# Attention division in two operations with its product on VectorE or ScalarE, the turned x of sequences 2 and 3 by DMA, the scale in the keys, and a new instruction order

## The chip, the cores and the metric

The kernel runs on one core of one Trainium2 chip. The metric is device time in microseconds (us). The kernel before takes 217.81 us, the median of 3 runs (217.51 to 218.0).

The engines of the core each work through a list of instructions in order and wait for one another at semaphores: PE (TensorE: matrix products and turns), DVE (VectorE), ACT (ScalarE), POOL (GpSimd) and SP (SyncE, which here only issues DMA transfers). PE's row PEld is its weight load, which overlaps its products. DMA transfers run on 16 DMA engines that all queues share: POOL's loads come through the queue q0, SP's transfers and transposes through q1.

## The reference

Eight sequences (B) of 576 rows, eight heads (H) of 64 columns. Keys and values are averaged over eight neighbouring rows, which leaves 72 of each (Sp). Attention of 576 queries on 72 keys gives x, and x goes through a feed-forward network with a gate:

```python
k_p = k.reshape(B, H, Sp, pool, D).mean(axis=3)
v_p = v.reshape(B, H, Sp, pool, D).mean(axis=3)
scores = scale * np.matmul(q, k_p.transpose(0, 1, 3, 2))      # scale = 1/8
attn = np.exp(scores - np.max(scores, axis=-1, keepdims=True))
attn = attn / (np.sum(attn, axis=-1, keepdims=True) + 1e-09)
x = np.matmul(attn, v_p)                    # heads side by side: [8, 576, 512]
...
h = np.maximum(x @ w_in, 0.0)               # [8, 576, 1024]
conv_out = sum(conv_w[k] * hp[:, k:k + S] for k in range(3))  # hp: h padded by a row at both ends
gate = 1.0 / (1.0 + np.exp(-conv_out))
out = (h * gate) @ w_out                    # [8, 576, 512]
```

Inputs and output are float32. The kernel loads in bfloat16 and multiplies in bfloat16 with sums in float32.

## The kernel before

The eight sequences stand in four groups: 0 and 1, 2 and 3, 4 and 5, 6 and 7. The 1152 rows of a group are cut into nine tiles of 128 rows, t = 0 to 8: tiles 0 to 3 are the first sequence's, tile 4 is half the one and half the other, tiles 5 to 8 are the second's. Group 0 has ten, since its tile 4 is cut in two (4 and 9). So there are 37 attention tiles.

**Preparation.** POOL issues the loads of q, k, v and the weights; SP issues the raw first loads of sequence 0. For sequences 0 and 1 PE averages the keys with a pool matrix of ones (`clear_pool_matrix`, L341, `build_pool_matrix`); for later groups VectorE halves the pair of keys three times (`pool_pair`, L439), and PE turns the sums (`turn_pair` with the constant `pick` of `build_pick`, L371; `turn_keys`, L463, with the identity matrix `ident`, for group 3). The sums over eight rows aren't divided here. Queries are turned by PE and copied to qT (`prep_q`, `copy_q`, L534); those of group 3 are turned by DMA. Values are halved three times on VectorE and widened (`prep_v`, L486) with a column of ones for each head.

**An attention tile** is a chain of operations that `add_att` (L1193) adds:
- `att_scores` (L563, L582 and L595): PE, 576 columns of scores into two PSUM banks.
- `att_max` (L608): VectorE, the maximum of each head, negated, out of PSUM (negm).
- `att_shift`: VectorE subtracts it (sd, L620); for group 0 PE does it in PSUM.
- `att_exp` (L646): ScalarE, exponential with the immediate scale 1/64 (1/8 for the average, 1/8 for the scores), into e.
- e is turned to eT: by PE and a copy on VectorE or ScalarE in groups 0 and 1 (`att_turn` L657, `att_copy` L671), by a DMA transpose on SP's queue in groups 2 and 3 (`att_send` L666).
- `att_values` (L682): PE, twelve products per tile into two PSUM banks; each head has 64 columns and one column with the sum of its row.
- `att_divide` (L691): VectorE, one operation of two instructions, the reciprocal of the eight sums (r, L695) and the product of the eight heads with it (x, L697).
- x is turned to xT: by PE and a copy in groups 0 and 1 (`att_turn_out` L714, `att_copy_out` L722), by a DMA transpose on SP's queue in groups 2 and 3 (`att_out` L706). The switch is `Graph.X_DMA = 4`, the first sequence whose x is turned by DMA.

**The network of a sequence.** `ffn_in` (L727): for each of eight blocks of 128 columns of h, two halves of 288 rows of four products each ("half in-products"); the first half needs the xT of the sequence's first three tiles, the second that of its third to fifth. `ffn_relu` (L736) on ScalarE writes hT. The convolution of three taps is made on PE with diagonal matrices (`ffn_conv` L889, then tanh on ScalarE, L914, and 1 + on VectorE, L925 and L927), or for some half sequences with taps on ScalarE (L862) and VectorE (L864), tanh (L869), and `ffn_tap_gate`: 1 + (L875) and the product with h (L876). `ffn_times` (L935) is that product for the others. `ffn_out` (L943) makes eight products per output tile of 128 rows, in two halves of four; `ffn_copy` (L954) copies the tile out of PSUM on VectorE or ScalarE into osb (in group 3 into old buffers of q, named qp), and `ffn_store` (L956) stores it.

**Buffers.** Fixed rings, among them: x four, r three, eT three, e six, osb five, xT two, q four, v three, keys of a pair (kk) one, and eight PSUM banks. A tile that takes a ring's buffer waits until the last reader of the tile before it in that buffer is done.

**What sets the order.** The code first adds all operations with their dependencies, the engines that each may run on and the buffers that it takes. Then `Graph.order` (L159) walks the table ORDER, written into the kernel: entry n means operation n // 2, on the first or the second of its engines (n % 2). FORMS gives the shape in which scores and turns are done, PLACES the slots of rings and PSUM banks. The instructions are issued in that order; on each engine they run in it, and across engines only the semaphores count. In the order before, the network starts with sequence 0, then 1, 3, 2, 4, 5, 6, 7. Its last product ends at 212.3 us of the profiled span.

Of the kernel before, what the change touches and what calls it, by code (L numbers as in the profile page):

```python
# [9 lines left out]
BF16 = mybir.dt.bfloat16  # L10
# [23 lines left out]
class Graph:  # L34
# [20 lines left out]
    X_DMA = 4  # L55
# [11 lines left out]
    SHIFT_PE = ((0, 0), (0, 1), (0, 2), (0, 3), (0, 4), (0, 5), (0, 6), (0, 7), (0, 8), (0, 9))  # L67
    TURN_DMA = 2
    BANKS = 8
    ORDER = (  # L70
# [107 lines left out]
def kernel(  # L178
# [10 lines left out]
    nc = tc.nc  # L189
# [12 lines left out]
    KW = 2 * Sp  # L202
    SLOTS = 24
    NJ = 5
    KP = NJ * P

    groups = [[0, 1], [2, 3], [4, 5], [6, 7]]
    where = {b: (g, i) for g, bs in enumerate(groups) for i, b in enumerate(bs)}
# [1210 lines left out]
```

## Time and profile before

| | |
|---|---|
| median of 3 runs | 217.81 us (217.51 to 218.0) |
| span of the profiled execution | 216.5 us |
| granted TensorE clock | 0.99 |
| busy: PE / DVE / ACT / POOL | 201.9 / 193.2 / 162.7 / 41.5 us |
| share of the span | 93 / 89 / 75 / 19% |
| HBM read, written | 32.52 MB, 9.44 MB |
| reciprocals, products (L695, L697), all on VectorE | 37, 37 |
| output copies (L954): ACT, DVE | 32, 5 |
| transposes by DMA: of e, of x | 18, 18 |

The profile is taken by the hardware on one execution. Its lines of groups give the line of the code, the engine, the operation and the tiles (out<-in, partitions x elements), the number of instructions, then the busy time in us and the mean of one instruction in ns, then the time that the engine idled just before them and what ended most of it. The chain of waits is followed back from the last instruction: each line gives a start and a length in us, the engine, the tile, the line and the number of instructions. A line of the timeline gives the start and the length of a piece of an engine's work in us. A line of a window gives its bounds and length, then the busy us and number of instructions of PE, PEld, DVE, ACT and POOL, the granted clock, the mean share of the 16 DMA engines and GB/s. A line of a DMA queue gives its packets, MB and the share of the window's DMA engine time that they took. A line of transposes gives the ns to issue one (shortest, median, longest), the first and the last issue in us; "to landing" is from issue to the last byte.

### The profile page before, as it was taken

To read this page: it belongs to the slowest core of one execution; us is meant where nothing else is said; L and a number is where in the kernel's file an instruction comes from. 1 tells how busy PE (TensorE), PEld (TensorE's weight loads), DVE (VectorE), ACT (ScalarE), POOL (GpSimd) and SP (SyncE) were. 2 spreads that over 40 slices of the span, in tenths; PEclk is the share of its full clock that TensorE was granted. 3 is DMA by queue.
4 is the path that set the end of the run, shared out by engine and by line. 5 is a ranking of instruction groups with operands and counts; after the bars stand their busy time and mean duration, and the time that the engine had idled before them with its cause. 6 is when DMAs were issued, how large, how long until landed. Compare 5 with 4: busy or idle time off the path is not lost.

```text
span 216.5 us, 6617 instructions
## 1 busy us (share of the span) xinstructions
PE 201.9 (93%) x2753; PEld 137.0 (63%) x2753; DVE 193.2 (89%) x334; ACT 162.7 (75%) x278; POOL 41.5 (19%) x78
## 2 busy tenths in 40 slices
PE   7599999969999999999999899989999999999992
PEld 3557778855788776766776675665656666654451
DVE  7598989999999999999999799999899999998621
ACT  2548885896998887787497594878979999997420
POOL 8644330050052101000000030002201210370000
PEclk9799999999999999999999999999999999999999
DMA  6999999999999999969687634576347745602685
GB/s 210 227 207 209 206 207 208 210 205 206 207 205 206 154 153 179 158 164 165 131 111 100 136 74 89 58 156 148 78 104 153 158 100 123 145 0 51 169 242 171
DMA packets 48833, 33.46 MB, mean 155 GB/s; under 512 B 28300, under 2 KB 43812, under 8 KB 48804
## 3 DMA queue, kind: packets, MB, share of 16 engines
q0 software_dynamic: 15216, 15.40, 43.5%
q1 hardware_dynamic: 32512, 16.13, 36.6%
q10 hardware_dynamic: 1076, 1.52, 2.5%
q8 instruction: 21, 0.34, 0.7%
q14 instruction: 8, 0.07, 0.1%
HBM read 32.52 MB, written 9.44 MB: 194 GB/s over the span
## 4 chain that ended last, share of the span: by engine, by line
PE 45%; DVE 34%; issue 6%; ACT 6%; DMA 5%; SPq 2%; DVEq 0%
PE psum L943 20%; PE psum L727 16%; DVE negm L608 7%; DVE x L697 6%; DVE sd L620 4%; DVE gT L935 4%; DMA hT<-in_k_dram 3%; DVE v L486 3%; DVE gT L927 3%; PE psum L889 2%; DMA out_dram<-osb 2%; DVE r L695 2%; PE psum L682 2%; ACT e L646 2%; DVE gT L925 1%
## 5 line engine op out<-in xcount | busy, mean ns | idle before, releaser
L727 PE MATMUL psum<-xT,w_in_sb 128*128 128x288 bf16 x512 | 74.1, 286 | 2.2 <-DMA xT<-x 1.1
L943 PE MATMUL psum<-w_out_sb,gT 128*128 128x512 bf16 (+1 forms) x296 | 69.5, 374 | 0.7 <-DVE gT L935 0.6
L727 PEld LDWEIGHTS <-w_in_sb 128*128 128x128 bf16 x512 | 47.9, 98 | 19.1 <-issue 2.0
L736 ACT ACTIVATE hT<-psum 128x576 bf16<-128x576 f32 x64 | 40.3, 650 | 14.0 <-PE psum L727 13.4
L943 PEld LDWEIGHTS <-gT 128*128 128x128 bf16 x296 | 27.3, 98 | 26.5 <-issue 0.9
L864 DVE SCALAR_TENSOR_TENSOR tg<-hT,convw,tg 128x576 f32<-128x576 bf16 x48 | 37.6, 815 | 0.5
L608 DVE TENSOR_REDUCE negm<-psum 128x8 f32<-128x576 f32 (+2 forms) x37 | 27.5, 752 | 2.3 <-PE psum L582 1.6
L697 DVE TENSOR_TENSOR x<-psum,r 128x512 bf16<-128x512 f32 (+1 forms) x37 | 25.6, 691 | 1.4
L811 POOL COPY hT<-hT 128x126 bf16<-128x126 bf16 x16 | 7.5, 467 | 97.6 <-ACT hT L736 80.1
L620 DVE TENSOR_TENSOR sd<-psum,negm 128x576 f32<-128x576 f32 x27 | 20.2, 753 | 0.5
L682 PE MATMUL psum<-vm,eT 128*128 128x130 bf16 (+5 forms) x240 | 18.9, 222 | 1.1 <-DVE x L697 0.7
L646 ACT ACTIVATE e<-sd 128x576 bf16<-128x576 f32 x27 | 18.2, 685 | 1.3 <-DVE sd L620 1.1
L954 ACT COPY osb<-psum 128x512 f32<-128x512 f32 x27 | 15.7, 585 | 4.4 <-PE psum L943 4.2
L889 PE MATMUL psum<-hT,dw 64*64 64x288 bf16 (+2 forms) x608 | 18.7, 261 | 0.1
L682 PEld LDWEIGHTS <-eT 128*128 128x128 bf16 (+1 forms) x240 | 15.3, 100 | 5.4 <-DMA eT<-e 1.2
L862 ACT ACTIVATE tg<-hT,convw 128x576 f32<-128x576 bf16 x24 | 18.1, 772 | 0.1
L889 PEld LDWEIGHTS <-dw 64*64 64x64 bf16 x608 | 14.8, 107 | 4.6 <-issue 3.7
L869 ACT ACTIVATE gT<-tg 128x576 bf16<-128x576 f32 x24 | 16.3, 683 | 0.7 <-DVE tg L864 0.5
L914 ACT ACTIVATE gT<-psum 128x576 bf16<-128x576 f32 x20 | 12.9, 651 | 3.9 <-PE psum L889 2.7
L914 ACT ACTIVATE tg<-psum 128x576 bf16<-128x576 f32 x20 | 13.0, 652 | 2.6 <-PE psum L889 1.4
L935 DVE TENSOR_TENSOR gT<-gT,hT 128x2304 bf16<-128x2304 bf16 x10 | 13.5, 1352 | 0.1
L486 DVE TENSOR_TENSOR v<-v 128x1280 bf16<-128x1280 bf16 (+2 forms) x24 | 13.0, 540 | 0.2
(84 smaller groups left out, 234.2 us busy)
## 6 DMA issues: line engine op xcount, KB each, us to landing
out_dram<-osb SPq DMA_DIRECT2D x54, 128.0 KB, 2.4
v<-in_v_dram POOLq DMA_DIRECT2D x8, 512.0 KB, 13.1
qp<-in_q_dram POOLq DMA_DIRECT2D x7, 576.0 KB, 14.4
kk<-in_k_dram POOLq DMA_DIRECT2D x3, 1152.0 KB, 14.6
out_dram<-qp ACTq DMA_DIRECT2D x10, 128.0 KB, 2.7
hT<-in_k_dram SPq DMA_DIRECT2D x2, 576.0 KB, 5.0
w_in_sb<-in_moe_w_in_dram POOLq DMA_DIRECT2D x2, 512.0 KB, 14.2
w_out_sb<-in_moe_w_out_dram POOLq DMA_DIRECT2D x1, 1024.0 KB, 24.7
```

The costliest lines, as they stand in the source:

```text
L608: nc.vector.tensor_reduce(out=a["m"][0:rows], in_=a["s"][0:rows, :, 0:2 * KW].rearrange("p a (h s) -> p a h s", s=Sp), axis=AX.X, op=OP.ma ...
L620: nc.vector.tensor_tensor(out=a["d"][0:rows], in0=a["s"][0:rows, :, 0:2 * KW].rearrange("p a (h s) -> p a h s", s=Sp), in1=a["m"][0:rows]. ...
L646: nc.scalar.activation(out=dst, in_=src, func=ACT.Exp, scale=1.0 / (POOL * 8.0),)
L682: nc.tensor.matmul(out=a["o"][lo:hi, h // 4, (h % 4) * (D + 1):(h % 4 + x1 - x0) * (D + 1)], lhsT=a["eT"][:, j, lo:hi], rhs=buf("vm", b)[: ...
L697: nc.vector.tensor_tensor(out=a["x"][0:rows].rearrange("p (a h d) -> p a h d", a=2, d=D), in0=ov[:, :, :, 0:D], in1=r[0:rows].unsqueeze(3) ...
L727: nc.tensor.matmul(out=banks(ps)[:, j, 0:SC], lhsT=w_in_block(dc, fb), rhs=buf("xT", g)[:, dc, i * S + j * SC:i * S + (j + 1) * SC], start ...
L736: nc.scalar.activation(out=h_of(b)[:, fb].rearrange("p (a s) -> p a s", a=2), in_=banks(ps)[:, :, 0:SC], func=ACT.Relu, scale=0.5,)
L864: nc.vector.scalar_tensor_tensor(out=acc, in0=h, scalar=w, in1=acc, op0=OP.mult, op1=OP.add)
L889: nc.tensor.matmul(out=banks(pss[r ^ c])[c * D:(c + 1) * D, j, lo:hi], lhsT=dw[r * D:(r + 1) * D, tap * n_fb + fb, :], rhs=hT[r * D:(r + 1 ...
L914: nc.scalar.activation(out=t.rearrange("p (a s) -> p a s", a=2), in_=banks(ps)[:, :, 0:SC], func=ACT.Tanh, scale=0.5,)
L935: nc.vector.tensor_tensor(out=gate, in0=gate, in1=h_of(b)[:, four], op=OP.mult)
L943: nc.tensor.matmul(out=bank(ps)[0:rows, columns], lhsT=buf("gT", g)[:, fb, t * P:t * P + rows], rhs=w_out_sb[:, fb, columns], start=(fb == 0),
```

## The change

- Division: `att_divide` becomes two operations that the order places on their own. `att_invert` is the reciprocal, on VectorE. `att_divide(g, t, engine)` is the product, on VectorE as before or on ScalarE as eight activations of 64 columns, one for each head, whose scale is read from a column of r. In the new order 20 products are VectorE's and 17 ScalarE's (136 activations).
- `X_DMA` goes from 4 to 2: the nine tiles of x of group 1 (sequences 2 and 3) are turned by DMA on SP's queue. There are 27 such transposes where there were 18; 36 turns on PE and nine copies go.
- The scale 1/64 goes into the keys: the pool matrix is set to 1/64 (`KSCALE`), and `build_pick` and `turn_keys` use a scaled identity, `ident_k`, that one more instruction on VectorE makes. The exponential has no scale.
- The 1 + and the product of `ffn_tap_gate` become two operations.
- `att_exp` gets a form with one activation per head (`Graph.EIGHT`); the table of tiles that use it is empty.
- An output tile of group 3 waits for the turned queries of sequences 4 to 7, where it waited for those of sequence 7.
- ORDER, FORMS and PLACES are new as a whole. The network still starts with the sequences 0, 1, 3, 2, 4, 5, 6, 7. On VectorE stand seven more output copies of 128x512 into osb and one into qp, two more copies of eT, one more of qT and three of kT in place of one, and one copy of xT where there were four; ScalarE has 24 full output copies where it had 32, and seven copies of xT where it had 13. The first raw loads are two of keys and then one of q, where q stood between the two of keys.

```diff
-    X_DMA = 4
+    X_DMA = 2
...
+    EIGHT = ()
...
     ORDER = (
...
+    KSCALE = 1.0 / (POOL * 8.0)
...
+    ident_k = const.tile([P, P], BF16, name="ident_k")
...
     def clear_pool_matrix():
-        nc.vector.memset(pm[0:TB, :, 0:Sp], 1.0)
+        nc.vector.memset(pm[0:TB, :, 0:Sp], KSCALE)
...
     def build_pick():
+        nc.vector.tensor_scalar(out=ident_k, in0=ident, scalar1=KSCALE, scalar2=None, op0=OP.mult)
         for hh in range(2):
             for f in range(2):
                 nc.vector.tensor_copy(
                     out=pick[:, hh].rearrange("p (s f a e) -> p s f a e", s=2, f=2, a=2)[:, :, f],
-                    in_=ident.rearrange("p (s a hh f e) -> p s a hh f e", s=2, a=2, hh=2, f=2)[:, :, :, hh, f],
+                    in_=ident_k.rearrange("p (s a hh f e) -> p s a hh f e", s=2, a=2, hh=2, f=2)[:, :, :, hh, f],
...
                     lhsT=buf("kk", g)[:, c, 0:D],
-                    rhs=ident[:, i * D:(i + 1) * D],
+                    rhs=ident_k[:, i * D:(i + 1) * D],
...
             func=ACT.Exp,
-            scale=1.0 / (POOL * 8.0),
         )
...
-    def att_divide(g, t):
+    def att_heads(g, t):
+        return att[g, t]["o"][0:rows_of(g, t), :, 0:4 * (D + 1)].rearrange("p a (h d) -> p a h d", d=D + 1)
+
+    def att_invert(g, t):
+        nc.vector.reciprocal(out=buf("r", g, t)[0:rows_of(g, t)], in_=att_heads(g, t)[:, :, :, D])
+
+    def att_divide(g, t, engine):
         a, rows = att[g, t], rows_of(g, t)
-        ov = a["o"][0:rows, :, 0:4 * (D + 1)].rearrange("p a (h d) -> p a h d", d=D + 1)
-        r = buf("r", g, t)
-        nc.vector.reciprocal(out=r[0:rows], in_=ov[:, :, :, D])
+        ov, r = att_heads(g, t), buf("r", g, t)
         a["x"] = buf("x", g, t)
+        if engine == "ACT":
+            for n in range(H):
+                nc.scalar.activation(
+                    out=a["x"][0:rows, n * D:(n + 1) * D],
+                    in_=ov[:, n // 4, n % 4, 0:D],
+                    func=ACT.Identity,
+                    scale=r[0:rows, n // 4, n % 4:n % 4 + 1],
+                )
+            return
         nc.vector.tensor_tensor(
...
     def ffn_tap_gate(b, f4):
...
         nc.vector.tensor_scalar(out=gate, in0=gate, scalar1=1.0, scalar2=None, op0=OP.add)
-        nc.vector.tensor_tensor(out=gate, in0=gate, in1=h_of(b)[:, four], op=OP.mult)
...
-            o = add({"PE": 0.26}, key, lambda b=b, t=t: turn_keys(b, t), after=[prev, c0], uses=[t, kk[g]], mode=HALF, count=36)
+            o = add({"PE": 0.26}, key, lambda b=b, t=t: turn_keys(b, t), after=[prev, picked], uses=[t, kk[g]], mode=HALF, count=36)
...
-        o = add(dve(0.2, 0.69), key, lambda: att_divide(g, t), after=[o], uses=[x, rr, big])
+        o = add({"DVE": 0.115}, key, lambda: att_invert(g, t), after=[o], uses=[rr, big])
+        o = add({"DVE": 0.61, "ACT": 0.82}, key, None, after=[o], uses=[x, rr, big])
+        o.emit = lambda o=o: att_divide(g, t, o.engine)
...
-            gated = add(dve(0.78, 1.39), w, lambda f4=f4: ffn_tap_gate(b, f4), after=tanh, uses=[htok[b], gtok[g]])
+            o = add(dve(0.78), w, lambda f4=f4: ffn_tap_gate(b, f4), after=tanh, uses=[gtok[g]])
+            gated = add(dve(1.39), w, lambda f4=f4: ffn_times(b, f4), after=[o], uses=[htok[b], gtok[g]])
...
-            osb, free = (token("late", g, t), qdone[7, 0]) if g == 3 else (token("osb", g, t), [])
+            osb, free = (token("late", g, t), [x for n in range(4, B) for x in qdone[n, 0]]) if g == 3 else (token("osb", g, t), [])
```

More of the change, by code (lines that the diff above doesn't have):

```diff
@@ L260, with by_head @@
     add = graph.add
+    def by_head(g, t):
+        return (g, t) in Graph.EIGHT
     def shift_by_dve(g, t):
@@ L640, in att_exp @@
         e = a["e"] = buf("e", g, t)
+        if by_head(g, t):
+            for n in range(H):
+                r, k = n // 4, n % 4
+                at = (k // 2 * 4 + r * 2 + k % 2 if a["by_rows"] else n) * Sp
+                nc.scalar.activation(
+                    out=e[0:rows, at:at + Sp],
+                    in_=a["s"][0:rows, r, k * Sp:(k + 1) * Sp],
+                    func=ACT.Exp,
+                    bias=a["m"][0:rows, r, k:k + 1],
+                )
+            return
         src = a["d"][0:rows].rearrange("p a h s -> p a (h s)") if shift_by_dve(g, t) else a["s"][0:rows, :, 0:2 * KW]
@@ L872, in ffn_tap_gate @@
         g, i = where[b]
-        four = slice(4 * f4, 4 * f4 + 4)
-        gate = buf("gT", g)[:, four, i * S:(i + 1) * S]
+        gate = buf("gT", g)[:, 4 * f4:4 * f4 + 4, i * S:(i + 1) * S]
         nc.vector.tensor_scalar(out=gate, in0=gate, scalar1=1.0, scalar2=None, op0=OP.add)
-        nc.vector.tensor_tensor(out=gate, in0=gate, in1=h_of(b)[:, four], op=OP.mult)
     def ffn_conv(b, f2, pss):
@@ L1209, in add_att @@
         o = add(dve(0.75), key, lambda: att_max(g, t), after=[o], uses=[ng, s])
-        if shift_by_dve(g, t):
+        if by_head(g, t):
+            o = add({"ACT": 0.9}, key, lambda: att_exp(g, t), after=[o], uses=[e, s, ng, lim])
+        elif shift_by_dve(g, t):
             sd = token("sd", g, t)
```

9 lines of the change are left out of this document (7 added, 2 removed), and 140 rows, old and new, of tables (ORDER, PLACES).

## The prediction

> **What bounds the kernel now.** I read the page first, then the chain of waits, then VectorE's order of time around the place that the change reworks, then the transfers there.
>
> ```profile
> span 216.5 us, 6617 instructions
> PE 201.9 (93%) x2753; PEld 137.0 (63%) x2753; DVE 193.2 (89%) x334; ACT 162.7 (75%) x278; POOL 41.5 (19%) x78
> PE 45%; DVE 34%; issue 6%; ACT 6%; DMA 5%; SPq 2%; DVEq 0%
> L697 DVE TENSOR_TENSOR x<-psum,r 128x512 bf16<-128x512 f32 (+1 forms) x37 | 25.6, 691 | 1.4
> ```
>
> Two engines share the chain. In order of time it is VectorE's until about 75 us and mostly VectorE's until 145 us; from there on nearly every piece is a product of TensorE:
>
> ```profile
> 144.72 0.51 PE psum L682 x6
> 165.39 0.86 PE psum L943 x4
> 166.25 0.49 PE psum L727 x4
> 195.55 0.86 PE psum L889 x24
> 199.10 13.16 PE psum L943 x68
> ```
>
> Four products of the second layer take 0.86, four of the first 0.49. The landmark that I count from is the first in-product of sequence 3, which needs the turned x of tiles 4 to 8 of group 1:
>
> ```profile
> 72.83 0.65 PE L727 MATMUL psum<-xT,w_in_sb 128*128 128x288 bf16 x4
> 73.32 0.39 PE L714 MATMUL psum<-ident,x 128*128 128x128 bf16 x4
> 74.04 0.40 PE L714 MATMUL psum<-ident,x 128*128 128x128 bf16 x4
> 75.24 0.66 PE L727 MATMUL psum<-xT,w_in_sb 128*128 128x288 bf16 x4
> ```
>
> It starts at 75.24. From there TensorE's list is 98 half in-products x 0.49 = 48.0, 64 half out-products x 0.86 = 55.0, the last tile's 1.8, 13 convolutions at about 0.85 = 11, 20 value products (three of them double) at about 0.4 = 9.2, and scores, turns, q and keys about 7: 132. Its last product ends at 199.10 + 13.16 = 212.3, so 137 us pass for 132 of work: 5 us of gaps. The rest to 216.5, 4.2 us, is the last copy and store. So behind 75 us TensorE's own list is nearly the time, and before it VectorE's is.
>
> **The change part by part.** The new order lists instructions per engine; prices are from the rows.
>
> Division. A reciprocal and its product stand like this now:
>
> ```profile
> 63.78 1.35 DVE L439 TENSOR_TENSOR kk<-kk 128x2304 bf16<-128x2304 bf16 x1
> 65.28 0.69 DVE L697 TENSOR_TENSOR x<-psum,r 128x512 bf16<-128x512 f32 x1
> 65.89 0.20 DVE L695 RECIPROCAL r<-psum 128x8 f32<-128x8 f32 x1
> 66.12 0.69 DVE L697 TENSOR_TENSOR x<-psum,r 128x512 bf16<-128x512 f32 x1
> 66.73 0.75 DVE L608 TENSOR_REDUCE negm<-psum 128x8 f32<-128x576 f32 x1
> 72.84 0.69 DVE L697 TENSOR_TENSOR x<-psum,r 128x512 bf16<-128x512 f32 x1
> 73.44 0.74 DVE L722 COPY xT<-psum 128x512 bf16<-128x512 bf16 x2
> ```
>
> The product begins 0.03 after the reciprocal's end, while L608 begins 0.08 before the product's end. An instruction that doesn't need the one ahead thus starts 0.11 sooner. Of 37 reciprocals, 24 no longer have their product right behind them: 24 x 0.11 = 2.7 us less. The Trainium skill's VectorE: DVE Perf Modes (Rules for kernel authors) says of chained VectorE operations that the drain happens regardless; by it the 2.7 would be nothing. These rows show an overlap of 0.08 that a dependent follower doesn't get, so I keep the 2.7.
>
> 17 products go to ScalarE as eight activations of 64 columns each. VectorE loses 17 x 0.61 (65.28 to 65.89) = 10.4 us. ScalarE has no row of 64 columns; the nearest:
>
> ```profile
> L736 ACT ACTIVATE hT<-psum 128x576 bf16<-128x576 f32 x64 | 40.3, 650 | 14.0 <-PE psum L727 13.4
> L862 ACT ACTIVATE tg<-hT,convw 128x576 f32<-128x576 bf16 x24 | 18.1, 772 | 0.1
> L431 ACT CAST kT<-psum 64x144 bf16<-64x144 f32 x2 | 0.5, 270 | 1.1 <-DVE kT L431 1.1
> 153.62 1.74 ACT L736 ACTIVATE hT<-psum 128x576 bf16<-128x576 f32 x3 [0.40 <-PE psum L727]
> 151.30 1.44 ACT L862 ACTIVATE tg<-hT,convw 128x576 f32<-128x576 bf16 x2
> ```
>
> 144 columns take 0.27 and 576 take 0.65, so 64 take about 0.20; followers start 0.105 before an end (three in 1.74); a scale read from a column adds 0.12 (772 against 650). Low end: overlap and no charge for the column, 0.095 each, 0.76 for eight. High end: no overlap, 0.32 each, 2.6. I take 0.20 + 0.12 - 0.105 = 0.215, 1.7 for eight, because L862 shows both the charge and the overlap (two in 1.44). The Trainium skill's ScalarE: Activation LUTs (What ACT_TABLE_LOAD costs) gives 186 ns plus 0.833 per column, 93 more for each pointer operand and 93 of overlap: 0.24 each, an estimate of 1.9 for eight and 17 x 0.2 = 3.4 us more on ScalarE than my price.
>
> Copies. VectorE's share of them stands so today:
>
> ```profile
> L954 DVE COPY qp<-psum 128x512 f32<-128x512 f32 (+1 forms) x5 | 2.9, 583 | 6.7 <-PE psum L943 6.7
> L671 DVE COPY eT<-psum 128x640 bf16<-128x640 bf16 x3 | 1.5, 484 | 0.4 <-ACT kT L431 0.4
> L722 DVE COPY xT<-psum 128x512 bf16<-128x512 bf16 x4 | 1.6, 415 | 0.0
> L534 DVE COPY qT<-psum 128x1152 bf16<-128x1152 bf16 (+2 forms) x7 | 4.7, 672 | 1.4 <-PE psum L520 1.3
> L458 ACT CAST kT<-psum 64x288 bf16<-64x288 f32 x8 | 3.1, 394 | 0.1
> L431 DVE CAST kT<-psum 64x144 bf16<-64x144 f32 x2 | 0.6, 312 | 2.6 <-PE psum L406 2.6
> ```
>
> It takes 8 output copies from ScalarE (0.58 less 0.08 each: +4.0), two more of e (0.40 each), two of keys (ScalarE's 0.39, as near as a row comes) and two of q ahead of the landmark, and loses three xT copies at 0.33. The scale in the keys costs one 128x128 operation more on VectorE in the start, about 0.1; the exponential's immediate scale goes, and it takes as long without. The first loads come as k, k, q instead of k, q, k. VectorE waits 2.6 us for the first keys and 1.3 for q (the last columns above), so this is worth from -2.6 to about +1.3; I take 0 and keep the ends for the range.
>
> Up to the landmark VectorE's list thus changes by -2.4 (four products), -1.1 (ten drains), -1.0 (xT copies), +0.8, +0.75 and +1.1 (copies of e, keys and q), and -1.1 by work that the new order moves across the landmark (three parts of a gate and some casts go behind it, a maximum and a shift come ahead): -3.0 in all. Since VectorE sets the pace there, the landmark would come at 75.2 - 3.0 = 72.2 if nothing else held it. Behind the landmark VectorE loses 5.6 us, TensorE 2.2 (two half in-products, turns of x and e, two scores): 130. ScalarE gains 11 products between 75 and 160 us:
>
> ```profile
> 75.00:160.00 85.00, 82.30 (x1219) 55.82 (x1210) 81.29 (x134) 65.71 (x113) 8.33 (x19) 1.00 0.74 125
> ```
>
> 65.7 + 11 x 1.7 - 2.4 (five copies gone) = 82 of about 83 us. It fits, with nothing to spare, so I leave TensorE's gaps at 5.
>
> x turned by DMA. Nine tiles of group 1 lose four TensorE products and a copy each and get a DMA transpose on SP's queue, at a time when POOL's loads fill the engines:
>
> ```profile
> q0 software_dynamic: 4016, 4.10, 122.8%
> 75.00:80.00 5.00, 4.86 (x57) 3.71 (x48) 4.84 (x9) 4.43 (x9) 0.43 (x1) 1.00 0.85 118
> L706 SPq DMA_TRANSPOSE xT<-x x18: 1188/1217/2322, 100.6 to 178.2; - x18
> DMA to landing us min/median/max: 2.4/2.5/4.5
> ```
>
> The first row is 50 to 70 us; the last two are today's transposes of x, all after the loads: 1.2 to issue, 2.5 to land. Only two transposes of e (640 packets of 256 bytes) meet the loads today:
>
> ```profile
> DMA to landing us min/median/max: 4.3/6.3/8.3
> q0 software_dynamic: 446, 0.43, 92.6%
> q1 hardware_dynamic: 411, 0.11, 27.8%
> ```
>
> The one issued at 81.0 landed after 8.3 us. From 84 to 87 us both queues moved about the same number of packets, some 137 per us. An x of 128x512 is 512 such packets: 3.7 us beside the loads, and a lone one lands after about 8.3 - 0.9 = 7.4.
>
> Now the places. SP gets tiles 2, 8, 3, 7, 5, 6, 4 in this order, and x has four buffers: tile 7 writes tile 2's, tile 6 tile 8's, tile 4 tile 3's, each only after that transpose has read it. So products of VectorE now wait for DMA. Tile 2 is issued at about 60.5 and lands at 67.9; tile 8, ready near 62.6 since the 1.27 of L439 now comes later, lands 3.7 later at 71.6; tile 3 at 75.3. VectorE reaches tile 6's product near 67 and waits to 71.6; behind it stand the pooling of group 2's keys, so the next load (the last keys) is held too. Tile 4's product follows tile 3 at 75.3. Ahead of its transpose tiles 7, 5 and 6 still drain. Low end for four: SP's 1.2 each, 80.1; high end: 3.7 each, 90.1. Loads are thinner then (share 0.85 instead of 1.23) and the last keys are held, so I take the low end: the landmark at 80. TensorE stands until then, and with it the scores of group 2 and the maxima behind them.
>
> Sum: 80 + 130 + 5 + 4.2 = 219.2 us of span. The median of 217.81 is 1.3 above the profiled span, so 220.5.
>
> **The rivals.** First, the transposes keep up: the place is the same, the price a landing of 2.5 to 4 us, and it decides once tile 4's x lands by about 73. For it: eight transposes may be on their way at once, and the second of the two loaded ones took 4.3. Against it: the 8.3, and the buffers that tie tile 6 to 8 and 4 to 3. Then 72.2 + 139.2 = 211.4, 212.7 with the 1.3: faster. The Trainium skill's DMA: Bandwidth & Descriptors (Specifications) gives about 0.6 us to the first byte on this path, which speaks for this case; no row here is that short under load.
>
> Second, loads stay dense through the drain: landmark 90, 230.5. Against it is the held load of the keys.
>
> Third, ScalarE becomes the bound between 75 and 160: at 2.6 per product 65.7 + 28.6 - 2.4 = 92, 9 us over, so 222 even if the transposes keep up. Against it is the overlap in every ScalarE row.
>
> Fourth, stall and savings cancel: the transposes drain at some 1.9 us each, between the two ends, and the landmark comes at about 77: 77 + 139.2 + 1.3 = 217.5.
>
> That the split doesn't save would add at most 1.1 ahead of the landmark; it lies inside the forecast's range.
>
> **How the numbers follow.** The forecast has 0.50 (216.5 to 226 alone), the first rival 0.30, the second 0.08, the third 0.05, the fourth 0.07. About 0.2% of 217.8, 0.4 us, is what a measurement here tells from no change. Faster: 0.30 + 0.04 of the fourth = 0.34; same: 0.02 of the forecast and 0.03 of the fourth = 0.05; slower: the rest, 0.61. The range takes in the first rival and the start's unknown 1.3 below it, and cuts the second: 211.5 to 226.5.
>
> **What would show it.** In the changed profile: transposes of x issued before 90 us that land after 4 to 8 us; VectorE idle before the product of x with a DMA as the releaser; TensorE idle 4 us or more before the first in-product of sequence 3, at about 80; eight-part products of 1.4 to 2.0 us on ScalarE. I am wrong if that landmark comes before 75, if VectorE never waits for those transposes, or if the time is made later, between 80 and 160, by ScalarE.

## The result, and the profile after

The changed kernel takes 233.82 us (median of 4 runs, 233.38 to 234.15), the kernel before 217.66 on the same chips: a ratio of 1.0746, with a 95% interval from 1.0724 to 1.0769. The profiled execution's span is 232.4 us instead of 216.5. Three of the kernels below (e8, and e14 and e18, which are the same program) have executions 2 to 6% longer than their shortest, so of these the shortest are compared.

From the page of the changed kernel, the span, the busy times and the chain of waits by engine, then by line:

```profile
span 232.4 us, 6863 instructions
PE 203.3 (87%) x2791; PEld 136.9 (59%) x2791; DVE 188.0 (81%) x328; ACT 179.8 (77%) x395; POOL 42.6 (18%) x78
PE 43%; ACT 32%; DVE 9%; DMA 8%; issue 6%; ACTq 0%; DVEq 0%
PE psum L759 12%; PE psum L973 11%; ACT x L722 10%; DMA xT<-x 6%; ACT hT L768 6%; PE psum L919 5%; ACT gT L901 4%; ACT tg L894 4%; PE psum L701 3%; ACT e L666 3%; ACT osb L984 2%; PE psum L408 2%; DVE tg L896 2%; DMA eT<-e 2%; PE psum L676 2%
```

Lines have moved: L714 is the reciprocal, L729 VectorE's product, L722 ScalarE's, L738 the DMA transpose of x, L759 the in-products, L919 the convolutions. VectorE had 34% of the chain and now has 9%; ScalarE had 6% and has 32%. The largest single item of ScalarE there is the product.

The landmark of the prediction, the first in-product of sequence 3, is at 87.03 instead of 75.24. From TensorE's and then VectorE's order of time (start, length, instruction, idle time before and its releaser):

```profile
72.89 0.45 PE L676 MATMUL psum<-ident,e 128*128 128x128 bf16 x5
78.98 1.66 PE L919 MATMUL psum<-hT,dw 64*64 64x288 bf16 x32 [5.64 <-DVE x L729]
81.37 1.87 PE L759 MATMUL psum<-xT,w_in_sb 128*128 128x288 bf16 x8
87.03 0.65 PE L759 MATMUL psum<-xT,w_in_sb 128*128 128x288 bf16 x4
```

```profile
70.29 0.20 DVE L714 RECIPROCAL r<-psum 128x8 f32<-128x8 f32 x1
70.40 0.76 DVE L629 TENSOR_TENSOR sd<-psum,negm 128x576 f32<-128x576 f32 x1
71.08 0.20 DVE L714 RECIPROCAL r<-psum 128x8 f32<-128x8 f32 x1
71.31 0.69 DVE L729 TENSOR_TENSOR x<-psum,r 128x512 bf16<-128x512 f32 x1
72.10 0.21 DVE L714 RECIPROCAL r<-psum 128x8 f32<-128x8 f32 x1
78.24 0.69 DVE L729 TENSOR_TENSOR x<-psum,r 128x512 bf16<-128x512 f32 x1 [5.92 <-DMA xT<-x]
78.84 2.14 DVE L448 TENSOR_TENSOR kk<-kk 128x2304 bf16<-128x2304 bf16 x2
```

A product of VectorE waits 5.92 us for a transpose of x, and TensorE waits 5.64 us for that product. By the order it is the product of tile 6, whose buffer has to be read by tile 8's transpose first. (The first four rows also show what the split saves: after a reciprocal an independent instruction starts after 0.11, its own product after 0.23.) The times at which the first in-product of each sequence starts, from the trace, place the loss:

| kernel | 0 | 1 | 3 | 2 | 4 | 5 | 6 | 7 | end of span |
|---|---|---|---|---|---|---|---|---|---|
| before | 27.5 | 57.3 | 75.2 | 101.8 | 117.5 | 134.6 | 159.9 | 176.3 | 216.5 |
| changed | 28.9 | 60.7 | 87.0 | 112.9 | 129.5 | 148.6 | 174.9 | 194.1 | 232.4 |
| later by | 1.4 | 3.4 | 11.8 | 11.1 | 12.0 | 14.0 | 15.0 | 17.8 | 15.9 |

So 3.4 us are lost before the turns of group 1, 8.4 in them, and 4.1 behind the landmark. Each row is one execution: six kernels below whose instructions are the changed kernel's up to there (e1, e3, e13, e14, e17, e18) start sequence 0 at 27.6 to 28.6 and sequence 1 at 59.4 to 60.4, so a difference of about 1 us is scatter. The windows of the changed kernel (bounds, length, busy of PE, PEld, DVE, ACT, POOL, granted clock, DMA share, GB/s) for the last of these:

```profile
75.00:160.00 85.00, 76.31 (x1182) 54.15 (x1181) 71.31 (x120) 67.20 (x164) 8.51 (x17) 0.96 0.82 133
135.00:150.00 15.00, 13.94 (x151) 8.33 (x149) 12.92 (x21) 14.15 (x46) 1.42 (x4) 1.00 0.46 95
150.00:165.00 15.00, 13.95 (x175) 9.61 (x174) 13.41 (x24) 14.97 (x34) 2.93 (x6) 1.00 0.61 117
165.00:180.00 15.00, 13.39 (x100) 7.81 (x98) 13.05 (x19) 14.58 (x36) 1.42 (x4) 1.00 0.63 130
180.00:195.00 15.00, 13.76 (x98) 8.61 (x97) 13.50 (x21) 14.94 (x38) 3.97 (x6) 1.00 0.55 123
```

From 150 to 195 ScalarE is the engine without a gap, 44.5 of 45 us, and TensorE has 41.1 where it had all 45 before:

```profile
150.00:165.00 15.00, 15.00 (x125) 8.89 (x124) 14.27 (x21) 13.23 (x24) 1.38 (x4) 1.00 0.51 109
165.00:180.00 15.00, 15.00 (x109) 9.51 (x107) 14.80 (x24) 14.33 (x26) 3.09 (x8) 1.00 0.59 127
180.00:195.00 15.00, 15.00 (x96) 9.14 (x94) 14.57 (x18) 14.83 (x26) 5.75 (x8) 1.00 0.38 88
```

Why do the transposes land late? The queues of the changed kernel, from 68 to 72 us, from 74 to 76 and from 78 to 80 (packets, MB, share of the DMA engines), with the transposes issued in the first of these and their time to landing:

```profile
q0 software_dynamic: 733, 0.76, 119.7%
xT<-x SPq DMA_TRANSPOSE x2, 9.8
```

```profile
q0 software_dynamic: 262, 0.30, 112.1%
q1 hardware_dynamic: 265, 0.07, 44.0%
```

```profile
q1 hardware_dynamic: 1347, 0.32, 118.4%
q0 software_dynamic: 31, 0.02, 7.2%
```

In the four microseconds from 68 to 72 two transposes were under way and SyncE's queue q1 moved no packet; GpSimd's loads moved 733. The transpose of tile 8, issued at 68.28, gets its first packet at 72.2, 3.9 us after its issue; the one ahead of it, issued at 64.05 with next to no load under way, got it after 1.3 and landed after 2.5. Once q1 has begun, the two queues move about as many packets each, 262 and 265 from 74 to 76. When the loads leave off, at 79, q1 is alone, and 1347 packets go in 2 us. Tile 8's transpose lands 9.9 us after its issue. The Trainium skill's DMA: Bandwidth & Descriptors (Queues, rings and completion order) says that each DMA engine takes turns between its queues packet by packet. The rows from 74 to 76 agree. What holds the first packet back beside the loads is not shown; it is so in other kernels too, 3.4 us for the transpose of e at 81.0 in the kernel before and 4.0 in e13.

### The profile page after: what moved, and what is told of

Read it like the earlier page. It is cut to its first block, busy times and chain, and to the rows that moved or that the text cites. A ratio compares the mean times of both kernels' runs of the same rounds, so it can differ in the third digit from the quotient of the medians.

```text
span 232.4 us, 6863 instructions
## 1 busy us (share of the span) xinstructions
PE 203.3 (87%) x2791; PEld 136.9 (59%) x2791; DVE 188.0 (81%) x328; ACT 179.8 (77%) x395; POOL 42.6 (18%) x78
## 4 chain that ended last, share of the span: by engine, by line
PE 43%; ACT 32%; DVE 9%; DMA 8%; issue 6%; ACTq 0%; DVEq 0%
PE psum L759 12%; PE psum L973 11%; ACT x L722 10%; DMA xT<-x 6%; ACT hT L768 6%; PE psum L919 5%; ACT gT L901 4%; ACT tg L894 4%; PE psum L701 3%; ACT e L666 3%; ACT osb L984 2%; PE psum L408 2%; DVE tg L896 2%; DMA eT<-e 2%; PE psum L676 2%
## 5 line engine op out<-in xcount | busy, mean ns | idle before, releaser
L759 PE MATMUL psum<-xT,w_in_sb 128*128 128x288 bf16 x512 | 72.3, 288 | 3.6 <-ACT osb L984 1.2
L973 PE MATMUL psum<-w_out_sb,gT 128*128 128x512 bf16 (+1 forms) x296 | 67.4, 373 | 1.0 <-DVE osb L984 0.8
L759 PEld LDWEIGHTS <-w_in_sb 128*128 128x128 bf16 x512 | 48.2, 98 | 19.8 <-issue 6.0
L973 PEld LDWEIGHTS <-gT 128*128 128x128 bf16 x296 | 28.0, 98 | 28.6 <-issue 1.7
L722 ACT ACTIVATE x<-psum,r 128x64 bf16<-128x64 f32 x136 | 29.9, 358 | 1.5 <-DVE r L714 1.3
L919 PE MATMUL psum<-hT,dw 64*64 64x288 bf16 (+2 forms) x608 | 20.4, 267 | 9.2 <-DVE x L729 5.6
L843 POOL COPY hT<-hT 128x126 bf16<-128x126 bf16 x16 | 9.5, 596 | 85.3 <-ACT hT L768 78.6
L919 PEld LDWEIGHTS <-dw 64*64 64x64 bf16 x608 | 16.3, 109 | 13.5 <-issue 12.8
L965 DVE TENSOR_TENSOR gT<-gT,hT 128x2304 bf16<-128x2304 bf16 x16 | 21.6, 1347 | 0.2
L701 PE MATMUL psum<-vm,eT 128*128 128x65 bf16 (+5 forms) x240 | 19.1, 226 | 1.0 <-DMA eT<-e 0.8
L729 DVE TENSOR_TENSOR x<-psum,r 128x512 bf16<-128x512 f32 (+1 forms) x20 | 13.6, 686 | 6.3 <-DMA xT<-x 5.9
L901 ACT ACTIVATE gT<-tg 128x576 bf16<-128x576 f32 x24 | 16.8, 713 | 1.9 <-DVE tg L896 1.8
L944 ACT ACTIVATE tg<-psum 128x576 bf16<-128x576 f32 x20 | 13.2, 658 | 4.8 <-PE psum L919 4.7
L313 POOL DMA_DIRECT2D v<-in_v_dram x8 | 6.1, 758 | 45.5 <-DVE vm L499 41.8
```

The costliest lines, as they stand in the source:

```text
L701: nc.tensor.matmul(out=a["o"][lo:hi, h // 4, (h % 4) * (D + 1):(h % 4 + x1 - x0) * (D + 1)], lhsT=a["eT"][:, j, lo:hi], rhs=buf("vm", b)[: ...
L722: nc.scalar.activation(out=a["x"][0:rows, n * D:(n + 1) * D], in_=ov[:, n // 4, n % 4, 0:D], func=ACT.Identity, scale=r[0:rows, n // 4, n ...
L759: nc.tensor.matmul(out=banks(ps)[:, j, 0:SC], lhsT=w_in_block(dc, fb), rhs=buf("xT", g)[:, dc, i * S + j * SC:i * S + (j + 1) * SC], start ...
L901: nc.scalar.activation(out=gate, in_=acc_of(b, fb, ps), func=ACT.Tanh, scale=0.5)
L919: nc.tensor.matmul(out=banks(pss[r ^ c])[c * D:(c + 1) * D, j, lo:hi], lhsT=dw[r * D:(r + 1) * D, tap * n_fb + fb, :], rhs=hT[r * D:(r + 1 ...
L944: nc.scalar.activation(out=t.rearrange("p (a s) -> p a s", a=2), in_=banks(ps)[:, :, 0:SC], func=ACT.Tanh, scale=0.5,)
```

## The experiments

Times are medians, with the ratio to the kernel before on the same chip. The diffs are shortened. The order was held by the tables of each kernel; only what the diffs show is different.

**e1: x of group 1 turned by TensorE in the new order.**

```diff
 for o in graph.order():
-    o.emit()                                  # att_out(1, t): DMA transpose on SP
+    att_turn_out(1, t, k)                     # k: a PSUM bank that is free there
+    att_copy_out(1, t, nc.vector.tensor_copy if t in (4, 5, 7) else nc.scalar.copy)
```

> The changed kernel, with the nine x of group 1 turned by TensorE and a copy again (VectorE copies tiles 4, 5, 7, ScalarE the others), all else as changed. Theory (the transposes beside the loads hold the landmark, the first in-product of sequence 3): the landmark comes from 87.0 to about 79, and the time falls by about 8 us, to 226. Rival (ScalarE sets the time behind the landmark anyway, so that what is won there is lost later): the landmark comes sooner, but the time stays within 2 us of 233.8.

233.08 us, 1.0693 [1.0634, 1.0753]. The landmark is at 84.8. The theory failed. The time is the rival's, but hardly for its reason: e10 below keeps behind the landmark what it wins ahead of it. What the transposes cost seems to come back as 36 turns and nine copies at places that the order wasn't made for; between 60 and 90 us TensorE's value products wait 2.7 us for ScalarE's copies of xT.

**e2: all products on VectorE in the new order.**

```diff
-        o.emit = lambda o=o: att_divide(g, t, o.engine)
+        o.emit = lambda o=o: att_divide(g, t, "DVE")
```

> The changed kernel with all 37 products on VectorE, at the same places of the order. Theory (ScalarE, busy over 14 of each 15 us between 135 and 195, costs the 4 us that are lost behind the landmark): ScalarE loses 29 us of work, VectorE gains 10.4, the landmark stays at 87 and the time falls by 3 to 5 us, to about 230. Rival (VectorE is as tight there): the time stays at 233.8 or rises, by up to 8.

236.00 us, 1.0809 [1.0751, 1.0866]: the rival. VectorE has no room for them in this order either.

**e3: the loads held until x is turned.**

```diff
+    if o is xdone[1, 4]:
+        nc.gpsimd.tensor_copy(out=gate_tile, in_=buf("xT", 1)[:, 0, 512:576])
+        held.emit()                           # the load of v 5; those of q 7 and q 6 follow
```

> The changed kernel in which GpSimd reads a piece of the turned x of tile 4 of group 1 before it issues the loads of the values of sequence 5 and of the queries of sequences 7 and 6, so that the seven transposes have the DMA engines to themselves. Theory (the loads keep the transposes waiting, up to 9.9 us): they land in 2.5 to 4 us, VectorE's wait of 5.9 goes, the landmark comes at about 80 and the time falls by 5 to 7 us unless the later loads are missed. Rival (SyncE's issue of 1.2 to 1.7 us each and the chain of the tiles set it): the landmark stays within 1.5 us of 87.

The transposes land in 2.4 to 4.1 us, and the landmark is at 79.3: the mechanism is as the theory had it. The time is 241.59, 1.1107 [1.1036, 1.1178], since the last keys now come behind the held loads. In the chain of waits of this kernel:

```profile
80.25 2.46 PE psum L760 x20
82.70 17.25 DMA kk<-in_k_dram
...
104.87 9.59 DMA eT<-e
```

**e4: both taken back** (e1 and e2 together).

> The changed kernel with both taken back: x of group 1 turned by TensorE and all products on VectorE; what is left is the new order, the split and the scale in the keys. Theory (two costs that add): 222 to 224, the rest over 217.7 being the 3.4 us that the new order is late before the first tile of group 1 is turned. Rival (one cost hides behind the other): within 1.5 us of the better of the two runs that take one back.

230.94 us, 1.0583 [1.0523, 1.0644]. Neither theory: the new order without the transposes and ScalarE's products, but with the split and the scale, is 13 us slower than the old one. The turns stand at the next places with a free PSUM bank, as in e1.

**e5 to e8: the parts in the old order.** The same edits on the kernel before; e8 is e5, e6 and e7 together.

```diff
-            o.emit = lambda o=o: att_copy_out(g, t, copier(o))
+            o.emit = lambda o=o: att_copy_out(g, t, copier(o)) if g == 0 else att_out(g, t)      # e5
...
+        if (g, t) in ACT17:                                                                       # e6
+            for n in range(H):
+                nc.scalar.activation(out=a["x"][0:rows, n * D:(n + 1) * D], in_=ov[:, n // 4, n % 4, 0:D],
+                                     func=ACT.Identity, scale=r[0:rows, n // 4, n % 4:n % 4 + 1])
+            return
```

> The kernel before, in its own order, with one part of the change: where the copy of the turned x of a tile of group 1 stood, SyncE issues its DMA transpose, and TensorE's four products are left out. Four runs of the changed order have shown that taking back parts of the change there wins 0 to 3 of 16 us. New theory (the new order is what costs, whatever its parts): this part alone costs at most 3 us in the old order. Rival (the transposes cost beside the loads in any order, and in the new one something else stands behind them): they land only when the loads end at about 74 and again after 76, the landmark comes at 81 or later, and the time rises by 5 us or more, to 223 or above.

> The kernel before, in its own order, with the same 17 products as in the change on ScalarE, as eight activations each, at their old places. ScalarE gains 17 x 1.75 = 29.8 us, VectorE loses 10.4. New theory (the order costs): at most 3 us. Rival (ScalarE costs in any order): it has 1.6 us free of 30 between 165 and 195 but 15 free of 60 between 105 and 165, so the time rises by 4 to 10 us.

> The kernel before, in its own order, with the scale 1/64 in the keys and none in the exponential. Both theories: no change (within 0.5 us); anything else would mean that the exponential without a scale, or the one more instruction of VectorE in the start, has a price of its own.

> The kernel before, in its own order, with x of group 1 by DMA, the 17 products on ScalarE and the scale in the keys: all parts of the change but the new order and the place of the reciprocal (here right ahead of its product). New theory (the order costs): at most 222, and so 12 us or more under the changed kernel. Rival (the parts cost, and the changed order was made to bear them): 230 or more, near the changed kernel or above it.

| kernel | us | ratio | landmark |
|---|---|---|---|
| e5, x by DMA | 230.53 | 1.0582 [1.0522, 1.0643] | 83.7 |
| e6, 17 products on ScalarE | 238.01 | 1.0924 [1.0858, 1.099] | 80.4 |
| e7, scale in the keys | 217.50 | 0.9988 [0.9967, 1.001] | 75.2 |
| e8, all three: the shortest of 4 | 245.26 (the others 252.72 to 258.91) | | 87.7 |

The scale is free. Of the other two the transposes cost 13 us in the old order, as their rival had it (though two of e5's land after 9.2 us, at 71.0 and 75.7, with the loads still running to 80), and the products 20, twice what their rival had; together they cost 28 in the shortest execution. So the parts cost in either order, and the new order bears them better, by 11 us (245.26 against 233.82); the new theory, that the order alone costs, is wrong. But e4 showed that the new order doesn't pay without them either.

**e9 to e11: the parts at the prices that the order was laid out for.** The new order's table reckons 0.82 us for a product on ScalarE (the diff shows it: `{"DVE": 0.61, "ACT": 0.82}`) and 1.29 us for the issue of a transpose and 1.4 more to its landing. e9 makes ScalarE's products shorter (each activation takes one head's sum for four heads), e10 leaves the transposes of group 1 out, so that they cost nothing at all, and e11 does both. What is left out is missing in their output.

```diff
-            for n in range(H):
+            for n in range(2):
                 nc.scalar.activation(
-                    out=a["x"][0:rows, n * D:(n + 1) * D],
+                    out=a["x"][0:rows, n * 4 * D:(n + 1) * 4 * D].rearrange("p (h d) -> p h d", d=D),
...
     def att_out(g, t):
+        if g == 1:
+            return
```

> The changed kernel, with ScalarE's products as two activations of 256 columns instead of eight of 64; each takes one head's reciprocal for four heads, so the division by the other heads' sums is left out. By the rows of 144 and 576 columns each takes some 0.4 to 0.5, a product 0.8 to 0.95 instead of 1.75, which is near the 0.82 that the new order's own table assumes; ScalarE loses 17 x 0.85 = 14 us. Theory (the new order was laid out for prices that the chip doesn't give): most of this comes off behind the landmark, total 222 to 227. Rival (the order itself is bad): 231 or more.

> The changed kernel without the nine transposes of x of group 1: they are left out, and xT of that group holds zeros, which GpSimd writes early. This is the order with transposes that cost nothing. Theory: VectorE's wait of 5.9 us and the wait for the last landing go, the landmark comes at 78 to 80, and the time falls by 5 to 8 us. Rival (the order is late anyway, as the run with TensorE's turns had it): 231 or more.

> The changed kernel with both: products on ScalarE in two activations of 256 columns and the nine transposes of x of group 1 left out (division by six heads' sums and the turned x of group 1 are missing). Theory (the new order at the prices that it was laid out for): at most 217, so that the order is as good as the old one once its two assumptions hold. Rival (the order itself is bad): 225 or more.

The product's group in e9, beside which the changed kernel's is 29.9 us for 136 instructions:

```profile
L722 ACT ACTIVATE x<-psum,r 128x256 bf16<-128x256 f32 x34 | 14.3, 481 | 1.7 <-DVE r L714 1.4
```

| kernel | us | ratio | landmark | landmark to end of span |
|---|---|---|---|---|
| changed | 233.82 | 1.0746 [1.0724, 1.0769] | 87.0 | 145.4 |
| e9, shorter products | 227.51 | 1.0438 [1.0366, 1.0509] | 84.1 | 142.2 |
| e10, no transposes | 225.93 | 1.0391 [1.0355, 1.0428] | 79.1 | 144.8 |
| e11, both | 217.00 | 0.9976 [0.9944, 1.0007] | 76.5 | 137.5 |

e10 and e11 win what their theories said. e9 stays half a microsecond above its theory's range, and of its 6.3 us only 3.2 come off behind the landmark. Together the two win 16.8 us: with short products and no transposes in group 1 the new order is as fast as the old one, and no faster.

**e12: the split alone, in the old order.**

```diff
         nc.vector.reciprocal(out=r[0:rows], in_=ov[:, :, :, D])
+        waiting.append((g, t))                # the product, out of this function
...
     for o in graph.order():
         o.emit()
+        if had and o.engine == "DVE":         # had: waiting, as it was ahead of this operation
+            att_times(*had[0])
```

> The kernel before in its own order, with the division as two operations: the product of VectorE is put behind the next instruction of VectorE after its reciprocal where the buffers allow it, else it stays. By the rows an instruction that doesn't need the one ahead starts 0.11 us sooner, some 30 x 0.11 = 3.3 us of VectorE's list, about half of it ahead of the landmark. Theory (the split saves a little): 215.5 to 217.5. Rival (each x comes later by the instruction in between, 0.2 to 1.3 us, and TensorE waits for it): 218 to 221.

230.46 us, 1.0587 [1.0549, 1.0625], worse than the rival. x comes an instruction later each time, and TensorE waits for it already in the start; two of its waits there, of 0.97 and 1.50 us, and the granted clock of 0.89 from 15 to 60 us (the kernel before has 1.00):

```profile
25.40 0.61 PE L722 MATMUL psum<-ident,x 128*128 128x128 bf16 x8 [0.97 <-DVE x L705]
28.01 0.69 PE L520 MATMUL psum<-ident,qp 64*64 64x64 bf16 x36 [1.50 <-DVE x L705]
```

```profile
15.00:60.00 45.00, 37.51 (x716) 28.53 (x715) 33.37 (x64) 29.02 (x49) 9.15 (x12) 0.89 1.20 199
```

**e13: x of group 1 in buffers of its own.**

```diff
+    buffers["x"] += [spare[:, 4096 + 512 * n:4608 + 512 * n] for n in range(7)]
+        x.own = 4 + t - 2 if g == 1 and t >= 2 else None
```

> The changed kernel in which x of tiles 2 to 8 of group 1 lies in seven buffers of their own (in the part of gT that is free at that time) instead of the ring of four. Theory (the landing is what costs, and the ring only shows it at another place): VectorE's wait of 5.9 us goes, the products are ready by 74, but the transposes still land only when the loads end at about 78, so the landmark comes at 82 to 85 and the time at 229 to 232. Rival (the four buffers are the cause, as the prediction had it): the landmark at 80 or before, the time at 227 or less.

236.81 us, 1.088 [1.078, 1.0981], worse than both. VectorE no longer waits for the transposes and TensorE works on to 80, so the keys of group 2 are done sooner, and with that GpSimd issues the next loads at 77, ahead of the last transpose at 79. TensorE's order of time and the queues from 80 to 86 us:

```profile
88.12 1.12 PE L764 MATMUL psum<-xT,w_in_sb 128*128 128x288 bf16 x4 [8.11 <-DMA xT<-gT]
```

```profile
q0 software_dynamic: 969, 0.99, 98.5%
q1 hardware_dynamic: 924, 0.23, 23.5%
```

The landmark is at 88.1. The stall at the four buffers had held those loads back; without it the stall only stands at another place. In e3, with the four buffers and the loads held, the landmark was at 79.3. So the landing beside loads is the cause, not the buffers.

**e14 and e18: TensorE kept busy in its stall.**

```diff
+    for _ in range(24):
+        fill(bank)                            # 448 columns of zeros, ahead of the convolution at 79.0
```

> The changed kernel with 24 products of zeros on TensorE (448 columns, about 0.21 us each, 5 us) ahead of the second convolution of sequence 1, where TensorE stands idle from 73.3 to 79.0 and then runs at half its clock until 82.6. Theory (the stall has a second price, the clock): the granted clock stays at 1.0, the work from 79 to 83 takes about 2 us less, the time falls by 1 to 3 us. Rival (VectorE and the transposes set the pace there anyway): within 0.7 us of 233.8.

> The kernel with 24 products of zeros in TensorE's stall once more, with more rounds, since its times fell apart (231.0, 231.1, 237.2, 238.8) while its profiled run was 3 us shorter than that of the changed kernel. Theory (the clock after the stall costs 1 to 3 us): a median of 230.5 to 232.8. Rival (no price of its own): 233 to 235 or more.

Medians of 234.17 and 237.49 over four and six runs, from 230.97 to 240.26; four of the ten lie between 230.9 and 231.8. The profiled execution of e14 has a span of 229.3, and its clock stays at 1.0, where the changed kernel's windows show half:

```profile
76.00:78.00 2.00, 0.00 (x0) 0.00 (x0) 0.00 (x0) 0.00 (x0) 0.00 (x0) 0.51 1.03 134
78.00:80.00 2.00, 1.02 (x24) 0.98 (x27) 1.76 (x2) 0.00 (x0) 0.00 (x0) 0.50 1.26 174
80.00:82.00 2.00, 2.00 (x31) 1.41 (x24) 1.41 (x5) 1.19 (x2) 0.00 (x0) 0.50 0.34 66
82.00:84.00 2.00, 2.00 (x35) 1.45 (x33) 1.05 (x3) 0.69 (x2) 0.00 (x0) 0.78 0.04 9
84.00:86.00 2.00, 1.41 (x50) 1.23 (x49) 1.70 (x4) 0.97 (x3) 1.78 (x3) 1.00 1.33 130
```

So the theory fits the four shortest runs, some 231.1 against 233.8, and the medians don't show it. What may differ is another race of the same kind. SyncE's turn of the queries of sequence 7 and GpSimd's load of the last keys fall within half a microsecond; from SyncE's order of time in the changed kernel, e14 and e18:

```profile
84.00 3.12 SPq L537 DMA_TRANSPOSE qT<-qp  x1
```

```profile
81.93 9.61 SPq L537 DMA_TRANSPOSE qT<-qp  x1
```

```profile
83.92 12.94 SPq L537 DMA_TRANSPOSE qT<-qp  x1
```

Issued 0.22 us ahead of the load it takes 3.12 us to issue, 0.50 behind it 9.61 or 12.94. Whether this sets which of the two times an execution has was not settled.

**e15 and e16: shorter products, and both cheap, in the old order** (the edits of e9 and e11 on the kernel before).

> The kernel before in its own order with the 17 products on ScalarE as two activations of 256 columns (division by the other heads' sums left out): ScalarE gains some 17 x 0.9 = 15 us instead of 29.8. Theory (price: what ScalarE gains is paid about two thirds in this order, as 20.4 of 29.8 were): 226 to 229. Rival (place: it is the wait for ScalarE at the old places that costs, not the length): 234 or more.

> The kernel before in its own order with all parts of the change at the prices that the new order assumes: products in two activations, the scale in the keys, and the turns of x of group 1 left out (xT holds zeros). The new order with these took 217.0. Theory (parts and order belong together): the old order is worse with them, 221 or more. Rival (the new order brings nothing of its own): 218 or less.

221.63 us, 1.0187 [1.0122, 1.0253], and 223.15, 1.027 [1.019, 1.035]. In e15 ScalarE's products take 14.4 us where e6 has 30.2; 16 us less on ScalarE are 16.4 us less of time. Length, not place, then, and paid in full, where the theory had two thirds and so 226 or more. And e16 is as its theory had it: in e16 the old order is 6 us slower with these parts than the new one with them (217.0): order and parts belong together.

**e17: the loads behind the turned x, nothing left out.**

```diff
+    nc.gpsimd.tensor_copy(out=gate_tile, in_=buf("xT", 1)[:, 0, 512:576])
     load_pair(3)
+    load_v(5); load q 7; load q 6             # were ahead of it; their turns go behind e of group 2
```

> The changed kernel with its loads put in another place of GpSimd's queue: the keys of group 3, the values of sequence 5 and the queries of 7 and 6, in this order, all behind the landing of the turned x of tile 4 of group 1 (GpSimd reads a piece of it first), and the DMA turns of those queries behind SyncE's last transpose of e of tiles 0 to 4 of group 2. Nothing is left out. Theory (the transposes cost by landing behind the loads): they land in 2.5 to 4 us, the landmark comes at 79 to 80 as in the run with the loads held, nothing behind it waits for the keys, and the time is near that of the order without these transposes, 225 to 228. Rival (the loads that come later are missed wherever they stand): 231 or more.

237.89 us, 1.0943 [1.0887, 1.1]: the rival. The transposes of x land in 2.4 to 4.3 us and the landmark is at 79.8, but now a transpose of e meets the moved loads. Its place in the chain of waits:

```profile
90.80 0.60 PE psum L760 x4
...
91.72 13.97 DMA eT<-e
...
105.74 1.49 PE psum L702 x12
```

The place of the loads only chooses which transposes wait. But e3 and e17 show what the landmark pays for: with no load beside them the transposes leave it at 79.3 and 79.8, and without any transposes (e10) it is at 79.1. No version found here is faster than the kernel before.

## Why the prediction was wrong

The direction and the stall were as forecast: VectorE waits for a DMA before a product of x, TensorE waits 5.6 us behind it, and the landmark is late. The time, 233.8, lies above the range. The span is 13.2 us over the sum, 7.0 of them ahead of the landmark and 6.2 behind it. Step by step:

- **"Since VectorE sets the pace there, the landmark would come at 75.2 - 3.0 = 72.2 if nothing else held it." This failed first.** With no transposes and short products (e11) it comes at 76.5, with no transposes and real ones (e10) at 79.1. VectorE's list did get shorter: in e11 it has 64.5 us of work by 75 us where the kernel before has 67.6, the 3 us of the forecast. But the engine waited more instead. Up to 60 us it was busy like this, in the kernel before and then in the changed one:

```profile
0.00:30.00 30.00, 25.17 (x419) 17.87 (x420) 24.45 (x63) 18.06 (x31) 15.16 (x31) 0.94 1.11 211
30.00:60.00 30.00, 27.79 (x506) 21.00 (x505) 28.43 (x50) 24.61 (x44) 5.04 (x7) 1.00 1.23 207
```

```profile
0.00:30.00 30.00, 22.68 (x461) 15.35 (x462) 22.09 (x63) 17.81 (x35) 14.66 (x27) 1.00 1.10 209
30.00:60.00 30.00, 27.36 (x508) 19.85 (x506) 26.51 (x45) 24.87 (x49) 4.41 (x6) 1.00 1.24 207
```

  VectorE did 52.9 us of work by 60 before and 48.6 after, and sequence 1 starts 3.4 us later. A list's sum is a bound, not a date: a new order has its own waits, 4.3 us here (76.5 less 72.2), and ScalarE's longer products cost another 2.6 ahead of the landmark (79.1 less 76.5). Which part of the new order makes the 4.3 stays open; in e11 VectorE's longest waits up to there are 1.9 us each, for value products and for scores.
- **The transposes: size right, but by luck.** The prediction put 7.8 us on them (72.2 to 80), and they cost 7.9 (87.0 less 79.1 in e10). Its places were right: tile 6's product waits for tile 8's transpose, and the wait holds the next loads back. Its times were not. It had tile 8 ready near 62.6 and landing 3.7 us behind tile 2, at 71.6; it was issued at 68.28 and landed at 78.15: a transpose that finds loads under way first waits 3.9 us for its first packet and only then shares. The later ones then went fast, tiles 6 and 4 in 2.4 to 2.5 us with the loads over, and the two errors made up for each other. e13 shows that the buffers weren't the cause.
- **"It fits, with nothing to spare, so I leave TensorE's gaps at 5." This failed next.** From landmark to end the forecast was 139.2; it is 145.4. The price was right: 1.7 per product was taken, and the trace has eight activations in 1.74 to 1.75. With short products and no transposes the same stretch takes 137.5; with the real products put back it takes 144.8, 7.3 more. An engine planned at 82 of 83 us among others that wait for it doesn't fit. That is nearest to the third rival, but at the price of the forecast and behind 135 us rather than ahead of it; its 0.05 was far too low.
- **The split.** An independent instruction does start 0.11 us after a reciprocal, as taken. But in the old order the split as e12 makes it costs 12.9 us, since x comes later.
- **The scale** costs nothing, as taken (e7). The start's new loads were not tried by themselves; with short products sequence 0 starts at 27.0 (e9) and 26.7 (e11), no later than the 27.5 of before, so they can't have cost much.
- **The fourth rival's 77** doesn't follow from its 1.9 us a transpose: six more at that pace from tile 2's landing at 67.9 are 79.3.

In the sum: 72.2 + 4.3 + 2.6 + 7.9 = 87.0, and 145.4 behind it. Against e11, with short products and no transposes in group 1, the changed kernel loses 2.6 + 7.9 ahead of the landmark and 7.9 behind it, 18.4 us of span. The terms are differences of single executions, each good to about 1 us. The prediction's sum had only the transposes.

## What to carry to other kernels

A frozen order is worth what its prices are worth: before a change of order is priced by sums of lists, compare the prices it was made for with the profile's rows (0.82 against 1.75 us, 2.7 against 9.9), for the same order with products at about its price and no transposes in group 1 was 16.8 us faster. A DMA transpose that is issued while large loads are under way should be booked with a wait for its first packet (3.4 to 4.0 us here) and then one packet for each of the loads', in all 8 to 10 us to the landing where its queue was empty; the loads needn't end first (in e13 one issued at 76.5 landed at 83.8, with loads until 92). In a kernel whose TensorE, VectorE and ScalarE are 75 to 93% busy, each part taken alone can cost many times its own length, so a single part in the old order doesn't tell what it costs in the new one.

## What the runs showed of the hardware that was not expected

- A transpose that was issued beside loads got its first packet only after 3.4 to 4.0 us (the kernel before, the changed one, e13), against 1.3 with no load under way. From then on both queues moved about as many packets, 262 and 265 in the changed kernel and 969 and 924 in e13 (80 to 86 us). What makes the wait was not found.
- The issue of a transpose can itself be held: the turn of 18 blocks took 3.12 us to issue just ahead of a load and 9.61 to 12.94 just behind one, and all of SyncE's queue stands behind it.
- After an idle time of TensorE from 73.3 the granted clock was 1.00 until 76, 0.51 from 76 to 78 and back at 1.00 from 84 on. The Trainium skill's TensorE: Matmul & The Clock Gate (Part 1) gives half rate after an idle window of about 3.4 us; the trace agrees with the halving, though it came 2.7 us after the last product.
- Activations of 64 columns last 0.35 us but follow one another every 0.20, so that the overlap is 0.15, where the prediction had 0.105.
